# A float32 square in block 0 written for GpSimd instead of ScalarE

## The chip, the cores and the metric

The kernel runs on one core of a Trainium2 chip. Its engines each take their own instructions in order: TensorE (PE in the profile, with its weight loads as PEld), VectorE (DVE), ScalarE (ACT), GpSimd (POOL) and SyncE (SP, which here issues the transfers). [...] The metric is the device time of one execution in microseconds (us), as the median of several.

## The reference

Attention of 8 batches (512 rows of x, 32 of state, 8 heads of 64) gives 4352 + 256 = 4608 rows of 512 numbers; two feed-forward layers follow. The change lies in the first of them:

```
def _moe_ref(x, w_in, w_out):        # x: 4608 x 512, w_in: 512 x 2048, w_out: 2048 x 512
    h = x @ w_in
    r = np.maximum(h, 0.0)
    g = r * r
    return g @ w_out
```

The second layer has an elu in place of the squared relu. The weights come as float64 and everything is computed to float32 accuracy: each product of two float32 matrices is made of three products of parts, a part HI rounded for TensorE and a rest LO = value - HI.

## The kernel before

The first layer runs block by block, one block being one batch (512 columns of x, transposed). Blocks 0 to 3 go through `s1_step` and `out_step`; blocks 4 to 7 and everything later go through other code, with products saved by sums of parts. A block has 16 steps f. In step f, `s1_x` makes h(f) from six matmuls of 128x512 into PSUM, `relu2` turns h(f) into the pair gs (HI and LO), and `out_step` takes the gs of two steps earlier (LAG = 2) as the moving side of twelve matmuls into the four accumulators `acc`. gs has three buffers, r and g have one each.

`relu2` (L583 to L591) has four instructions: L585, ScalarE, r = relu(h) out of PSUM; L587, ScalarE, g = r squared, float32; L589, ScalarE, gs[HI] = r squared, rounded; L590, VectorE, gs[LO] = g - gs[HI].

Block 0 is special, since the weights are turned from float64 to float32 beside it (`convert`, L222 to L241). The 8 pieces of w1 and 8 of v1 each have a tile of 128x1024: ScalarE makes the high part (L232) and the low part (L234) out of the loaded words, a clamp follows (L237: on VectorE for w1, on GpSimd for v1 but its first piece), then VectorE shifts (L238) and adds the low part (L241). Pieces of v1 are then split into HI (L260 on ScalarE or L258 on VectorE) and LO (L262 on VectorE). Three pieces are done before the first step, the other 13 are spread over steps 0 to 14. The converted w1 is wanted by `emit_m` (products with the state into m, split by L177 and L178) and the converted v1 by `out_step`. The attention of batch 1 is worked on beside it too (L392 to L506, L527 to L542).

What one engine does in which order is settled when the program is built: a scheduler orders the instructions by their dependences, with the conversions of a step tied to its relu by `pace`, so that a change of one line can move its neighbours. On the chip each engine then goes through its list in order.

## Time and profile before

| | us |
|---|---|
| median of 3 runs (1308.95 to 1310.94) | 1310.32 |
| the profiled execution, whole | 1313.85 |
| its span from first to last instruction | 1312.1 |
| TensorE busy in the span | 1292.2 |
| VectorE busy | 945.4 |
| ScalarE busy | 835.5 |
| GpSimd busy | 8.8 |

"Busy" is the time in which an engine had at least one instruction in work. TensorE is busy nearly all the time, so what counts is where it isn't. About 25 us of the span go by before the first step; block 0's conversions fill the stretch from 25.7 to 97.2 us. Instruction records on one engine overlap by some 0.08 us, as the next one starts while the last one drains.

### The profile page before, as it was taken

What the parts mean: (1) busy time and instruction counts of PE and PEld (TensorE: products, weight loads), DVE (VectorE), ACT (ScalarE), POOL (GpSimd) and SP (SyncE); (2) the same over time, 40 slices, a digit from 0 to 9 for tenths busy, and PEclk for the clock granted to TensorE, in tenths of its full rate; (3) what the DMA queues carried; (4) which work ended last, traced back from release to release, by engine and by line L of the source; (5) the groups of instructions that cost most, each with busy time, mean ns of one, the idle gap of its engine ahead of it and who ended that gap; (6) DMA issues with size and microseconds to landing.
All of it is one profiled execution on the core that took longest, in us unless ns stands there. A gap on an engine that the chain in (4) does not pass through costs nothing.

```text
span 1312.1 us, 19392 instructions
## 1 busy us (share of the span) xinstructions
PE 1292.2 (98%) x6964; PEld 1036.4 (79%) x6964; DVE 945.4 (72%) x1327; ACT 835.5 (64%) x1347; POOL 8.8 (1%) x13
## 2 busy tenths in 40 slices
PE   7989999999999999999999999999999999999999
PEld 5667777777677777779988888888888888888898
DVE  6996968687769865985767963789546984568644
ACT  6886778677765667665577644685446743666444
POOL 0110000000000000000000000000000000000000
PEclk9999999999999999999999999999999999999999
DMA  9889888786825653589686678767786777678733
GB/s 370 312 301 336 314 288 303 260 302 234 276 96 156 192 186 117 178 281 360 216 261 195 201 209 264 224 191 211 221 276 194 208 210 233 200 211 282 227 103 110
DMA packets 135408, 305.39 MB, mean 233 GB/s; under 512 B 14352, under 2 KB 28688, under 8 KB 132240
## 3 DMA queue, kind: packets, MB, share of 16 engines
q1 hardware_dynamic: 135312, 304.14, 70.9%
q8 instruction: 56, 0.92, 0.3%
q14 instruction: 40, 0.33, 0.1%
HBM read 227.54 MB, written 76.55 MB: 232 GB/s over the span
## 4 chain that ended last, share of the span: by engine, by line
PE 85%; DVE 5%; issue 5%; DMA 2%; ACT 2%; POOL 1%; POOLq 0%; SPq 0%; DVEq 0%; ACTq 0%
PE x L43 19%; PE X L43 13%; PE z L43 10%; PE Z L43 7%; PE y L43 4%; PE h L170 4%; PE h L172 4%; PE h L171 4%; PE acc L170 3%; PE Y L43 3%; PE acc L172 3%; PE acc L171 3%; PE as L43 2%; PE mp L362 2%; PE hs L43 1%
## 5 line engine op out<-in xcount | busy, mean ns | idle before, releaser
L178 DVE TENSOR_TENSOR gp<-g,gp 128x512 fp32r<-128x512 f32 (+1 forms) x224 | 212.4, 955 | 107.1 <-ACT gp L177 106.1
L177 ACT ACTIVATE gp<-g 128x512 fp32r<-128x512 f32 (+1 forms) x224 | 187.7, 843 | 155.6 <-PE x L43 78.2
L43 PE MATMUL x<-gp,wr 128*128 128x512 f32 x1152 | 272.7, 391 | 1.0 <-ACT eu L71 1.0
L43 PEld LDWEIGHTS x<-gp,wr 128*128 128x128 f32 x1152 | 215.1, 188 | 51.6 <-ACT eu L71 2.9
L43 PE MATMUL X<-xf,wr 128*128 128x512 f32 x768 | 186.6, 390 | 0.0
L43 PEld LDWEIGHTS X<-xf,wr 128*128 128x128 f32 x768 | 143.5, 188 | 31.5 <-ACT u L957 1.1
L43 PE MATMUL z<-gp,wr 128*128 128x512 f32 x576 | 133.5, 390 | 0.0
L43 PEld LDWEIGHTS z<-gp,wr 128*128 128x128 f32 x576 | 108.0, 188 | 23.4 <-issue 0.8
L953 DVE SCALAR_TENSOR_TENSOR g<-r,g 128x512 f32<-128x512 f32 x96 | 63.9, 689 | 62.8 <-ACT r L952 62.8
L170 PE MATMUL acc<-gs,v 128*128 128x512 f32 x256 | 103.9, 406 | 4.1 <-DVE gs L590 3.4
L170 PE MATMUL h<-at,m 128*128 128x512 f32 x256 | 101.8, 398 | 0.7 <-ACT m L177 0.7
L172 PE MATMUL h<-at,m 128*128 128x512 f32 x256 | 99.8, 392 | 1.5 <-DVE m L178 1.5
L171 PE MATMUL acc<-gs,v 128*128 128x512 f32 x256 | 100.1, 391 | 0.0
L171 PE MATMUL h<-at,m 128*128 128x512 f32 x256 | 99.9, 390 | 0.0
L172 PE MATMUL acc<-gs,v 128*128 128x512 f32 x256 | 99.4, 392 | 0.4 <-DVE v L262 0.4
L43 PE MATMUL Z<-xf,wr 128*128 128x512 f32 x384 | 97.4, 389 | 0.0
L951 ACT ACTIVATE r<-g 128x512 f32<-128x512 f32 x96 | 57.6, 625 | 58.6 <-DVE g L1001 41.6
L81 DVE TENSOR_TENSOR g<-g,g 128x1024 f32<-128x1024 f32 x72 | 87.5, 1220 | 0.8
L43 PEld LDWEIGHTS Z<-xf,wr 128*128 128x128 f32 x384 | 72.1, 188 | 15.0
L952 ACT ACTIVATE r<-r 128x512 f32<-128x512 f32 x136 | 81.6, 621 | 0.7
L170 PEld LDWEIGHTS acc<-gs,v 128*128 128x128 f32 x256 | 48.0, 188 | 31.4 <-issue 10.1
L43 PE MATMUL y<-gp,wr 128*128 128x512 f32 x288 | 68.6, 389 | 0.0
(166 smaller groups left out, 1994.7 us busy)
## 6 DMA issues: line engine op xcount, KB each, us to landing
wr<-f_v SPq DMA_DIRECT2D x288, 256.0 KB, 3.0
wr<-f_w SPq DMA_DIRECT2D x224, 256.0 KB, 3.0
f_v<-wf SPq DMA_DIRECT2D x40, 512.0 KB, 3.6
raw_w<-in_w_dram SPq DMA_DIRECT2D x32, 512.0 KB, 5.3
raw_v<-in_v_dram SPq DMA_DIRECT2D x32, 512.0 KB, 6.5
f_w<-wf SPq DMA_DIRECT2D x24, 512.0 KB, 3.7
wr<-p_v SPq DMA_DIRECT2D x48, 256.0 KB, 3.5
xt<-in_xt_dram SPq DMA_DIRECT2D x8, 1024.0 KB, 6.0
```

The lines of the kernel that those rows point to most:

```text
L43: nc.tensor.matmul(ps, wk[a], xk[b], start=start and k == 0 and i == 0, stop=last and k == len(w) - 1 and i == 2, skip_group_check=True)
L81: return lambda jj: tt(out=out[jj], in0=a[jj], in1=b[jj], op=ALU.subtract)
L170: mm(ps, w[HI], x[LO], start=first, stop=False)
L171: mm(ps, w[HI], x[HI], start=False, stop=False)
L172: mm(ps, w[LO], x[HI], start=False, stop=last)
L177: copy = nc.scalar.activation(out=hi, in_=src, func=AF.Copy)
L178: lows[:] = [nc.vector.tensor_tensor(out=lo, in0=src, in1=hi.bitcast(F32), op=ALU.subtract)]
L362: mm(ps[e][32 * k:32 * k + 32, :], st_t[b][r, k, :], x(k, r), start=True, stop=True)
L951: act(out=r, in_=h, func=AF.Relu, scale=-1.0)
L952: act(out=r, in_=r, func=AF.Exp, scale=-1.0)
L953: nc.vector.scalar_tensor_tensor(out=out, in0=r, scalar=-1.0, in1=h, op0=ALU.add, op1=ALU.max)
```

## The change

`relu2` is told its block. In block 0 the float32 square g is no longer ScalarE's: GpSimd multiplies r by r. ScalarE keeps the rounded square gs[HI], and VectorE's subtraction takes g from GpSimd. Blocks 1 to 3 are as before. Behind the new lines all line numbers are 3 higher (L589 becomes L592, L590 becomes L593).

```diff
-        def relu2(ps, n):
+        def relu2(ps, n, b):
             r = g_p.tile([P, n], F32, name="r", tag="r")
             pace[:] = [nc.scalar.activation(out=r, in_=ps, func=AF.Relu)]
             g = g_p.tile([P, n], F32, name="g", tag="g")
-            nc.scalar.activation(out=g, in_=r, func=AF.Square)
+            if b:
+                nc.scalar.activation(out=g, in_=r, func=AF.Square)
+            else:
+                nc.gpsimd.tensor_tensor(out=g, in0=r, in1=r, op=ALU.mult)
             gs = gs_p.tile([P, 2, n], F32R, name="gs", tag="gs")
             nc.scalar.activation(out=gs[:, HI], in_=r, func=AF.Square)
             nc.vector.tensor_tensor(out=gs[:, LO], in0=g, in1=gs[:, HI].bitcast(F32), op=ALU.subtract)
...
-            waiting.append((b, f, relu2(ps, S)))
+            waiting.append((b, f, relu2(ps, S, b)))
```

On ScalarE, at step 1 of block 0 (cv and raw_v are a piece of v1; a wait on Pool_49 is one for GpSimd):

```order
-L585 ACTIVATE r<-h 128x512 [waits PE_49,Activation_49]
+L585 ACTIVATE r<-h 128x512 [waits PE_49,Activation_49,Pool_49]
 L232 ACTIVATE cv<-raw_v_154 128x1024 [waits DMAHW2_49,DMAHW0_49]
-L587 ACTIVATE g<-r 128x512 [waits DVE_49,Activation_49]
-L589 ACTIVATE gs<-r 128x512
+L592 ACTIVATE gs<-r 128x512 [waits Activation_49]
 L234 ACTIVATE raw_v_154<-raw_v_154 128x1024
```

The square L587 is gone from the row between L232 and the rounded square, and the next relu now waits for GpSimd to have read r.

On VectorE, at steps 1 and 2 of block 0 (cv is a piece of v1, w_3 one of w1):

```order
+L593 TENSOR_TENSOR gs<-g,gs 128x512 [waits Activation_49,Pool_49]
 L238 TENSOR_SCALAR cv<-cv 128x1024 [waits Pool_49]
-L590 TENSOR_TENSOR gs<-g,gs 128x512 [waits Activation_49]
+L542 COPY stf<-srt_435 64x4x32 [waits PE_49]
 L241 ISA cv<-raw_v_154,cv 128x2048 [waits DMAHW0_49,DMAHW2_49,DVE_49,Activation_49]
-L542 COPY stf<-srt_435 64x4x32 [waits PE_49]
-L237 TENSOR_SCALAR w_3_429<-w_3_429 128x1024 [waits Activation_49]
+L593 TENSOR_TENSOR gs<-g,gs 128x512 [waits Activation_49,Pool_49]
+L237 TENSOR_SCALAR w_3_429<-w_3_429 128x1024
```

The subtraction waits for GpSimd as well as for ScalarE, and it stands ahead of the shift L238, which waits for GpSimd's clamp, and not behind it.

On GpSimd, the start of its list in the changed kernel (before, the clamps L237 stand there alone, seven in a row):

```order
+L590 TENSOR_TENSOR g<-r 128x512 [waits Activation_49]
+L590 TENSOR_TENSOR g<-r 128x512 [waits DVE_49,Activation_49]
+L237 TENSOR_SCALAR cv<-cv 128x1024 [waits Activation_49]
+L590 TENSOR_TENSOR g<-r 128x512 [waits DVE_49,Activation_49] x2
+L237 TENSOR_SCALAR cv<-cv 128x1024 [waits Activation_49]
```

Sixteen squares now stand among the seven clamps, most often two squares and then a clamp; each square waits for r from ScalarE and for VectorE to have read the last g.

## Rows read from the trace of the kernel before

**Rows 1.** The page: busy time, share of the span and instructions of each engine.

```profile
PE 1292.2 (98%) x6964; PEld 1036.4 (79%) x6964; DVE 945.4 (72%) x1327; ACT 835.5 (64%) x1347; POOL 8.8 (1%) x13
```

**Rows 2.** Busy time by stretch: stretch, length, engines, granted clock, DMA share, GB/s.

```profile
core 0: us, PE busy (x) PEld busy (x) DVE busy (x) ACT busy (x) POOL busy (x), PEclk, DMA share, GB/s
25.70:97.20 71.50, 66.10 (x452) 45.76 (x451) 64.65 (x87) 65.11 (x94) 8.13 (x7) 1.00 0.87 315
97.20:1312.10 1214.90, 1207.34 (x6402) 977.02 (x6400) 865.72 (x1218) 756.39 (x1234) 0.00 (x0) 1.00 0.70 225
```

**Rows 3.** Waits from 25.7 to 97.2 us: who for whom, total, times, longest.

```profile
PE acc L170 <- DVE gs L590: 3.4, 6, 1.2
PE srt L540 <- DVE m L178: 0.9, 1, 0.9
PE acc L172 <- DVE v L262: 0.4, 1, 0.4
PE h L172 <- DVE m L178: 0.4, 1, 0.4
PE acc L170 <- ACT v L260: 0.3, 1, 0.3
...
DVE cv L238 <- POOL cv L237: 4.6, 5, 1.3
DVE w L237 <- ACT w L232: 1.4, 1, 1.4
DVE gs L590 <- ACT gs L589: 0.3, 1, 0.3
```

**Rows 4.** ScalarE's groups, same stretch: count, busy us, mean ns, idle before.

```profile
L587 ACT ACTIVATE g<-r 128x512 f32<-128x512 f32 x15 | 9.7, 644 | 0.1
```

**Rows 5.** GpSimd in order of time: start, us, instruction, idle before it.

```profile
32.19 1.04 POOL L237 TENSOR_SCALAR cv<-cv 128x1024 f32<-128x1024 f32 x1 [30.89 <-ACT cv L232]
...
59.73 1.04 POOL L237 TENSOR_SCALAR cv<-cv 128x1024 f32<-128x1024 f32 x1 [7.48 <-ACT cv L232]
73.77 1.88 POOL L237 TENSOR_SCALAR cv<-cv 128x1024 f32<-128x1024 f32 x1 [12.99 <-ACT cv L232]
82.86 1.04 POOL L237 TENSOR_SCALAR cv<-cv 128x1024 f32<-128x1024 f32 x1 [7.22 <-ACT cv L232]
```

**Rows 6.** VectorE in order of time, around 59.7 and 73.8 us.

```profile
59.50 1.21 DVE L490 TENSOR_REDUCE m<-t 128x32 f32<-128x1024 f32 x1
...
73.55 1.18 DVE L241 CUSTOM_DVE_ANT_0 w<-raw_w,w 128x2048 uint16<-128x2048 uint16 x1
74.76 1.42 DVE L590 TENSOR_TENSOR gs<-g,gs 128x512 fp32r<-128x512 f32 x1
```

**Rows 7.** VectorE's groups by form from 25.7 to 97.2 us.

```profile
L590 DVE TENSOR_TENSOR gs<-g,gs 128x512 fp32r<-128x512 f32 x14 | 10.3, 739 | 0.5 <-ACT gs L589 0.3
L262 DVE TENSOR_TENSOR v<-cv,v 128x1024 fp32r<-128x1024 f32 x8 | 9.8, 1220 | 0.0
L241 DVE CUSTOM_DVE_ANT_0 cv<-raw_v,cv 128x2048 uint16<-128x2048 uint16 x8 | 9.8, 1219 | 0.1
L241 DVE CUSTOM_DVE_ANT_0 w<-raw_w,w 128x2048 uint16<-128x2048 uint16 x6 | 7.3, 1212 | 0.0
L238 DVE TENSOR_SCALAR cv<-cv 128x1024 int32<-128x1024 int32 x8 | 5.5, 692 | 4.6 <-POOL cv L237 4.6
...
L238 DVE TENSOR_SCALAR w<-w 128x1024 int32<-128x1024 int32 x6 | 4.1, 690 | 0.1
L237 DVE TENSOR_SCALAR w<-w 128x1024 f32<-128x1024 f32 x6 | 4.1, 686 | 1.5 <-ACT w L232 1.4
...
L258 DVE CAST v<-cv 128x1024 fp32r<-128x1024 f32 x2 | 1.3, 672 | 0.0
...
L501 DVE TENSOR_TENSOR t<-t,z 128x1024 f32<-128x1024 f32 x1 | 1.2, 1225 | 0.0
L491 DVE TENSOR_TENSOR t<-t,m 128x1024 f32<-128x1024 f32 x1 | 1.2, 1218 | 0.0
```

**Rows 8.** ScalarE in order of time, step 1 of block 0.

```profile
30.45 0.61 ACT L585 ACTIVATE r<-h 128x512 f32<-128x512 f32 x1
30.92 1.18 ACT L232 ACTIVATE cv<-raw_v 128x1024 f32<-128x1024 f32 x1
31.97 0.66 ACT L587 ACTIVATE g<-r 128x512 f32<-128x512 f32 x1
32.49 0.65 ACT L589 ACTIVATE gs<-r 128x512 fp32r<-128x512 f32 x1
```

**Rows 9.** VectorE in order of time, the last subtractions of block 0.

```profile
102.26 0.69 DVE L590 TENSOR_TENSOR gs<-g,gs 128x512 fp32r<-128x512 f32 x1 [1.55 <-ACT gs L589]
106.34 0.69 DVE L590 TENSOR_TENSOR gs<-g,gs 128x512 fp32r<-128x512 f32 x1 [3.39 <-ACT gs L589]
```

## The prediction

> **What bounds the kernel now.** I read the page first: TensorE is busy 98% of the span, every other engine far less [rows 1], so a change away from TensorE can only matter where TensorE stands still. The busy time by stretch shows where that is [rows 2]. From 97.2 us to the end TensorE is idle 1214.9 - 1207.34 = 7.6 us in 1215; from 25.7 to 97.2 us, which is block 0 with the conversion of the weights, it is idle 71.5 - 66.1 = 5.4 us, at full clock (1.00). The squares that the change moves all lie in block 0. In that stretch three engines are nearly equally full: TensorE 66.1, ScalarE 65.1, VectorE 64.65 of 71.5 us. GpSimd has 8.1 us of work. Whichever of the three is made slower by a few us sets the stretch, and what is lost there is not won back, because TensorE has no slack behind it.

> Next the waits of the same stretch [rows 3]. TensorE waits for VectorE: 3.4 us for the subtraction L590, 0.9 and 0.4 for m, 0.4 for v; for ScalarE only 0.3. VectorE in its turn is idle 71.5 - 64.65 = 6.85 us, and the large waits behind that are 4.6 us for GpSimd's clamp, 1.4 for ScalarE's L232 and 0.3 for ScalarE's rounded square. So the last link before TensorE is VectorE, and ScalarE's lateness reaches TensorE only through VectorE's 6.3 us of waits.

> **What is removed.** ScalarE loses L587 in each of the 16 steps; 15 of them lie in the stretch with 9.7 us of records [rows 4], and a square moves its successor by 0.52 us (L589 starts 0.52 after L587 [rows 8]), so in 14 steps some 14 x 0.52 = 7.3 us of ScalarE's time. That cannot shorten the stretch by 7.3: TensorE has only 5.4 us to give, and VectorE, the last link, gains at most its 6.3 us of waits.

> **What is added, alone.** GpSimd gets 16 products of 128x512. None is in the trace. The nearest row is its clamp of 128x1024, 1.04 us when undisturbed [rows 5]: that reads 1024 numbers per partition, and a product of two 512-long inputs reads as many. Below, half of it (0.52) if r counted once; above, two passes like the clamp's (2.08). I take 1.04, the row with the same number of reads. [...] GpSimd then has 8.1 + 14 x 1.04 = 22.7 us in 71.5: it is not itself full.

> **What is added, beside VectorE.** One clash in the trace shows that the two engines don't run freely beside each other. At 73.77 the clamp starts while VectorE is in L241 (73.55, 1.18); the clamp takes 1.88 instead of 1.04, and the L590 that comes at 74.76 takes 1.42 [rows 5, 6] where 0.69 is usual [rows 9]. So the clamp stood until L241 was through and L590 stood until the clamp was through: 0.84 lost on one side, 0.73 on the other. At 59.73 a clamp runs beside L490, a reduction with one input, and both keep their time (1.04, 1.21) [rows 5, 6]. So GpSimd shuts out VectorE's operations with two inputs in SBUF and is shut out by them; one-input ones at the slow rate are free.

> How much of VectorE's time is of the excluding kind [rows 7]? The groups of the stretch add up to 69.7 us of records for 64.65 of busy time, a factor 0.93. With two SBUF inputs: L590 10.3, L262 9.8, L241 9.8 and 7.3, L491 and L501 1.2 each, 39.6 in all, so 36.7 us. The quick one-input operations L238 (5.5, 4.1), L237 (4.1) and L258 (1.3) are 15.0, so 13.9 us. No clamp meets one of these in the rows. They pass 1024 numbers in 0.69 us, where the reduction L490 needs 1.21, so they read at the rate of a two-input operation, and I count them as excluding. The rest is 15 us of records: reductions, transposes and L178, which has one input in PSUM. [...]

> So GpSimd finds VectorE in an excluding operation for (36.7 + 13.9) / 71.5 = 0.71 of the time, or 36.7 / 71.5 = 0.51 if the quick ones don't count. Each square that lands there costs VectorE about its own length. Of 16 squares 14 lie in the stretch; the last two fall where VectorE waits 1.55 and 3.39 us for its input [rows 9], and cost nothing. The term: 14 x 1.04 x 0.71 = **10.3 us** of VectorE (7.5 with the smaller share).

> **What moves.** VectorE's list has the subtraction ahead of the shift L238, no longer behind it. That uses part of the 4.6 us in which VectorE stood waiting for a clamp [rows 3]. Against it, a clamp now queues behind a square on GpSimd: in step 1, r is ready at 31.06 and L232, which releases the clamp, at 32.10 [rows 8], 1.04 later, exactly a square that starts at once; whatever a square is held up, the clamp behind it is late by, and with it L238 and L241. Also the square waits for VectorE to have read the last g (one buffer), and the relu for GpSimd to have read r; I take both as free, since each of the two is done within the step. Of VectorE's 6.3 us of waits I let half go, **3.2 us**: all of it is the bound if ScalarE's lead reaches every clamp, none if the squares eat the lead. No transfer is removed or added; those that wait for converted tiles come earlier or later with them.

> **Sum.** 10.3 - 3.2 = +7.1 us of VectorE. Before, VectorE's 64.65 us of work and 6.85 of idle made 71.5; now about 75 of work and blocked time and 3.7 idle make 78.6, while TensorE still wants 66.1 and ScalarE falls to some 58. VectorE becomes the bound of block 0, and the 7.1 pass on to the end. The profiled execution of 1313.85 would become 1320.9. It lay 3.5 above the median of the runs, 1310.32; on the median the forecast is 1317.4. The term's ends: with the smaller share and all waits recovered 7.5 - 6.3 = +1.2; with two-pass squares 20.7 - 3.2 = +17.5.

> **Rivals.**
> 1. ScalarE was the true bound, and GpSimd fits in between. For it: ScalarE is as full as VectorE (65.1), it feeds the clamps for which VectorE waits 4.6 us, and VectorE's new order puts gs earlier, which is what TensorE waits for (3.4 us). It needs squares that mostly hit VectorE's idle and free time. Against it: the clash. Its price is a gain of most of TensorE's 5.4 us idle, about 4: 1306.3. It decides if VectorE's blocked time stays below what its waits shrink by.
> 2. Both cancel: the smaller share (7.5) against all of the waits (6.3), or squares that fall into time in which VectorE waits for g anyway. Within 2.6 us of 1310.3.
> 3. Slower still: GpSimd gets no turn between back-to-back VectorE operations. In the clash L241 was followed by a VectorE pause for its input, so the rows don't show who wins when the next operation is ready. If VectorE always does, a square starts only when VectorE stands at the subtraction that wants it, and each costs its whole 1.04 and a start of some 0.09 (from the end of L232 at 32.10 to its clamp at 32.19 [rows 5, 8]): 14 x 1.13 = 15.8, less 3.2: +12.6, 1322.9. It decides if squares show as 2 us and more, with VectorE idle before L593.

> **How the numbers follow.** The forecast, slower by some 7 us, has 0.48, its own range is 1311.5 to 1322; rival 1 has 0.20, rival 2 0.18, rival 3 0.14. What a measurement can tell from no change here is about 0.2%, 2.6 us. Slower by more: 0.45 of the forecast's 0.48 (its lower end lies within the 0.2%) and all of rival 3, 0.59. Within: 0.18 + 0.03 = 0.21. Faster: 0.20. The range from 1306 to 1325 leaves out half of rival 1 and a part of rival 3.

> **What would show it.** In the profile after: GpSimd's squares with a median well over 1.04 us; L593, L241, L262 and L238 with longest records over 1.2 to 2 us and a larger mean; VectorE's busy time in block 0 near 75 us and its waits for GpSimd larger, now before L593; ScalarE at about 58; TensorE's idle time in block 0 near 12 us, and the time from block 1 on unchanged. I am wrong if squares and VectorE keep their undisturbed lengths, or if TensorE's idle time there falls below 5.4.

## The result: slower by 0.9%, as forecast in kind

The changed kernel takes 1321.76 us (median of four runs, 1319.86 to 1325.09), the kernel before 1309.88 us in the same comparison (1308.95 to 1310.94). The ratio is 1.0093 with a 95% interval of 1.0074 to 1.0111: 11.9 us slower, where 7.1 us were forecast and 1306 to 1325 us was the range. A second set of runs of the same kernel, below, gave 1319.35 us and 9.5 us. So the sign and the stretch were right, and the size was too small by 2.4 to 4.8 us.

The profiled execution took 1319.86 us with a span of 1317.9 us; that of before had 1313.85 and 1312.1. By the page, TensorE is still the engine that is always busy, GpSimd has 25 us more of records, and ScalarE has 7.8 us less, against [rows 1]:

```profile
PE 1294.6 (98%) x6964; PEld 1037.3 (79%) x6964; DVE 957.0 (73%) x1327; ACT 827.7 (63%) x1331; POOL 33.8 (3%) x29
```

The next rows are the busy times of stretches of the changed kernel: start and end, length, then each engine with its instructions, the granted clock, the DMA share. The first is the stretch of [rows 2]. Since the work of block 0 now takes longer, the same clock time holds less of it (TensorE 60.74 us for 66.10), so the stretch to compare ends at the first copy of block 0's accumulator: 121.59 us here, 111.62 before. The third row is what follows it.

```profile
25.70:97.20 71.50, 60.74 (x343) 42.02 (x341) 66.08 (x76) 51.13 (x69) 26.79 (x18) 0.93 0.75 272
...
25.70:121.59 95.89, 84.93 (x526) 59.42 (x525) 81.83 (x99) 63.66 (x90) 33.12 (x23) 0.95 0.79 285
...
121.59:1317.90 1196.31, 1191.21 (x6328) 964.50 (x6326) 860.05 (x1206) 749.96 (x1223) 0.00 (x0) 1.00 0.69 225
```

The same stretches of the kernel before:

```profile
25.70:111.62 85.92, 80.52 (x526) 56.75 (x525) 70.33 (x99) 71.63 (x107) 8.13 (x7) 1.00 0.88 319
...
111.62:1312.10 1200.48, 1192.91 (x6328) 966.03 (x6326) 860.05 (x1206) 749.88 (x1223) 0.00 (x0) 1.00 0.70 224
```

Block 0 ends 10.0 us later. VectorE has the same 99 instructions and needs 81.83 us for them instead of 70.33: 11.5 us more, all of it time in which an instruction stood. Its idle time shrank from 15.6 to 14.1 us. ScalarE fell by 8.0 us. TensorE's idle time rose from 5.4 to 11.0 us, and its busy time by 4.4 us, of which some 3.2 go with the granted clock (0.95 for 1.00): the same kernel at full clock, further below, has 81.75 us for 84.93. Behind block 0 nothing changed that can be told from the spread of single executions: 1196.3 us here, 1200.5 in the profiled execution of before, which was a long one (1313.85 against a median of 1309.88), and 1195.5 to 1200.4 in the ten other profiles of this document in which blocks 1 to 3 are as before.

Waits of the changed kernel from 25.7 to 97.2 us, answering [rows 3]: who for whom, us in total, times, longest.

```profile
PE acc L170 <- DVE gs L593: 2.8, 3, 1.8
...
PE acc L172 <- DVE v L262: 2.6, 2, 1.4
...
DVE v L262 <- ACT v L260: 2.3, 1, 2.3
...
PE mp L362 <- DVE w L241: 1.8, 2, 1.2
PE acc L170 <- DVE v L258: 1.7, 1, 1.7
...
POOL g L590 <- DVE gs L593: 1.4, 2, 0.7
...
DVE gs L593 <- POOL g L590: 0.9, 1, 0.9
```

VectorE no longer waits for clamps (4.6 us before), and it waits for squares only 0.9 us here (2.0 to the end of block 0). It waits less than before and works more slowly; and TensorE now waits for everything that VectorE makes, the converted tiles v and w (L262, L258, L241) as much as the subtraction.

How it becomes slow is seen in GpSimd's groups (count, busy us, mean ns), against clamps of 1.04 us undisturbed [rows 5]:

```profile
L590 POOL TENSOR_TENSOR g<-r 128x512 f32<-128x512 f32 x16 | 21.3, 1329 | 77.7 <-ACT r L585 72.3 <-DVE tf L276 3.3 <-DVE gs L593 2.1
L237 POOL TENSOR_SCALAR cv<-cv 128x1024 f32<-128x1024 f32 x7 | 12.0, 1719 | 0.0
```

and in GpSimd and VectorE in order of time (start, us, instruction). GpSimd:

```profile
30.53 2.13 POOL L590 TENSOR_TENSOR g<-r 128x512 f32<-128x512 f32 x1 [2.03 <-ACT r L585]
32.64 2.01 POOL L237 TENSOR_SCALAR cv<-cv 128x1024 f32<-128x1024 f32 x1
...
60.81 1.04 POOL L590 TENSOR_TENSOR g<-r 128x512 f32<-128x512 f32 x1 [2.18 <-ACT r L585]
...
76.90 1.04 POOL L590 TENSOR_TENSOR g<-r 128x512 f32<-128x512 f32 x1 [13.60 <-ACT r L585]
```

VectorE at the same moments:

```profile
30.55 1.22 DVE L262 TENSOR_TENSOR v<-cv,v 128x1024 fp32r<-128x1024 f32 x1
31.68 2.06 DVE L241 CUSTOM_DVE_ANT_0 w<-raw_w,w 128x2048 uint16<-128x2048 uint16 x1
33.67 1.52 DVE L593 TENSOR_TENSOR gs<-g,gs 128x512 fp32r<-128x512 f32 x1
...
60.86 1.53 DVE L258 CAST v<-cv 128x1024 fp32r<-128x1024 f32 x1
...
76.94 2.08 DVE L501 TENSOR_TENSOR t<-t,z 128x1024 f32<-128x1024 f32 x1
```

### The profile page after: what moved, and what is told of

Read it like the earlier page. It is cut to its first block, busy times and chain, and to the rows that moved or that the text cites. A ratio compares the mean times of both kernels' runs of the same rounds, so it can differ in the third digit from the quotient of the medians.

```text
span 1317.9 us, 19404 instructions
## 1 busy us (share of the span) xinstructions
PE 1294.6 (98%) x6964; PEld 1037.3 (79%) x6964; DVE 957.0 (73%) x1327; ACT 827.7 (63%) x1331; POOL 33.8 (3%) x29
## 4 chain that ended last, share of the span: by engine, by line
PE 83%; DVE 4%; DMA 2%; ACT 2%; issue 1%; SPq 0%; ACTq 0%; DVEq 0%
PE x L43 19%; PE X L43 13%; PE z L43 10%; PE Z L43 7%; PE y L43 4%; PE h L170 4%; PE h L172 4%; PE h L171 4%; PE Y L43 3%; PE acc L170 3%; PE acc L172 3%; PE acc L171 3%; PE as L43 2%; PE mp L362 2%; PE hs L43 1%; DMA f_v<-wf 1%
## 5 line engine op out<-in xcount | busy, mean ns | idle before, releaser
L178 DVE TENSOR_TENSOR gp<-g,gp 128x512 fp32r<-128x512 f32 (+1 forms) x224 | 212.4, 955 | 106.3 <-ACT gp L177 105.4
L170 PE MATMUL acc<-gs,v 128*128 128x512 f32 x256 | 104.8, 409 | 5.3 <-DVE gs L593 2.8
L172 PE MATMUL acc<-gs,v 128*128 128x512 f32 x256 | 101.3, 400 | 2.6 <-DVE v L262 2.6
L171 PE MATMUL acc<-gs,v 128*128 128x512 f32 x256 | 100.9, 394 | 0.0
L170 PEld LDWEIGHTS acc<-gs,v 128*128 128x128 f32 x256 | 48.6, 190 | 33.1 <-issue 11.7
L585 ACT ACTIVATE r<-h 128x512 f32<-128x512 f32 x64 | 38.0, 594 | 51.6 <-PE h L172 51.6
```

Source lines behind the costliest of these rows:

```text
L170: mm(ps, w[HI], x[LO], start=first, stop=False)
L171: mm(ps, w[HI], x[HI], start=False, stop=False)
L172: mm(ps, w[LO], x[HI], start=False, stop=last)
L178: lows[:] = [nc.vector.tensor_tensor(out=lo, in0=src, in1=hi.bitcast(F32), op=ALU.subtract)]
L585: pace[:] = [nc.scalar.activation(out=r, in_=ps, func=AF.Relu)]
```

## Experiments: does what GpSimd reads set the price?

My theory was that the time lost is VectorE's time shut out by GpSimd's reads of SBUF, the on-chip memory (the expectations call it a shared port, a name for the theory: the runs show lengths of instructions, not a port); the rival was that the new order and the new dependency (the subtraction waits for GpSimd) cost it, whatever the instruction does. The first two kernels have VectorE's, ScalarE's, TensorE's and SyncE's instructions in the order of the changed kernel; only GpSimd's instruction differs. The first keeps the dependencies, too; in the second GpSimd no longer waits for r, nor ScalarE's relu for GpSimd. The rows quoted below are always the stretch from 25.7 us to the first copy of block 0's accumulator.

**One read instead of two.**

```diff
-                nc.gpsimd.tensor_tensor(out=g, in0=r, in1=r, op=ALU.mult)
+                nc.gpsimd.tensor_scalar(out=g, in0=r, scalar1=CLAMP, scalar2=-CLAMP, op0=ALU.min, op1=ALU.max)
```

> GpSimd's instruction in block 0 clamps r into g (a one-input operation of the same kind as its clamp of the weights) where the changed kernel multiplies r by r; it leaves out the float32 square, and the lists of the four other engines stay word for word those of the changed kernel. Theory (the read port that GpSimd and VectorE share): what costs is the time in which GpSimd reads, so an instruction of 512 reads, about 0.52 us undisturbed, blocks VectorE half as long; 14 x 0.52 x 0.71 = 5.2 us less 3.2 of waits: 1 to 6 us above the kernel before, against 11.9 for the changed kernel. Rival (the new order of VectorE's list and the hand-over between three engines cost the time): nothing of that changes, so about 12 us stay.

1316.15 against 1310.21 us, ratio 1.0049 [1.0034, 1.0064]: 5.9 us slower, half of the change's 11.9.

```profile
25.70:118.33 92.63, 84.05 (x528) 59.30 (x527) 77.47 (x100) 63.77 (x90) 25.90 (x23) 0.96 0.81 295
```

**No read at all.**

```diff
-                nc.gpsimd.tensor_tensor(out=g, in0=r, in1=r, op=ALU.mult)
+                nc.gpsimd.memset(g, 0.0)
```

> GpSimd's instruction in block 0 fills g with zeros, without reading r; it leaves out the float32 square, and the lists of the four other engines stay word for word those of the changed kernel. Theory (shared read port): an instruction that reads nothing doesn't hold VectorE's two-input operations, so VectorE keeps its lengths (means near 0.69 and 1.22 us), and what is left is the relief of ScalarE: from 4 us faster than the kernel before to 2 slower. Rival (order and hand-over): about 12 us slower, as the changed kernel.

1313.16 against 1310.21 us, ratio 1.0023 [1.0013, 1.0032]: 2.95 us slower, a little above my range, far from the rival's 12.

```profile
25.70:113.52 87.82, 81.50 (x528) 57.00 (x527) 74.93 (x100) 63.63 (x91) 25.51 (x22) 1.00 0.86 312
```

**The product twice.**

```diff
                 nc.gpsimd.tensor_tensor(out=g, in0=r, in1=r, op=ALU.mult)
+                nc.gpsimd.tensor_tensor(out=g, in0=r, in1=r, op=ALU.mult)
```

> The changed kernel with GpSimd's product made twice into the same g. Theory (shared port): another 14 x 1.04 x 0.7 = 10 us of blocked VectorE, so 20 to 26 us above the kernel before, with more time at the lower granted clock. Rival (order and hand-over): the second product only lengthens the way to g, for which two steps of lag have room: 12 to 15 us.

1333.47 against 1310.21 us, ratio 1.0183 [1.0167, 1.0200]: 23.3 us slower.

```profile
25.70:134.51 108.81, 87.89 (x526) 60.19 (x525) 86.97 (x99) 64.02 (x90) 57.50 (x39) 0.92 0.70 254
```

The kernels together: with 0, 512, 1024 and 2048 numbers read per partition and step, the kernel is 2.95, 5.9, 9.5 to 11.9 and 23.3 us slower than before, and VectorE's busy time in block 0 is 74.93, 77.47, 81.4 to 81.8 and 86.97 us. Undisturbed, the memset and the clamp of r are of nearly one length (0.53 and 0.61 us), and the one that reads costs twice as much. The rival wanted 12 us from both; it falls with the clamp of r, whose order and dependencies are those of the change.

Only up to 1024 does the price follow the reads, though. Against the two profiles of the change the second product adds 5.1 to 5.5 us to VectorE's busy time, but 7.8 to 9.2 us to its idle time (108.81 - 86.97 = 21.8 us, after 14.1 and 12.6): the subtraction now waits for the second product, 10.3 us in block 0 after 2.0 and 2.3. So more than half of what the second product costs is the hand-over that the rival named.

## Experiments: what the relief and the order are worth

**No square at all.** The subtraction reads r, and neither engine makes g.

```diff
-                nc.gpsimd.tensor_tensor(out=g, in0=r, in1=r, op=ALU.mult)
+                g = r
```

> Block 0 has no float32 square at all: VectorE subtracts the rounded square from r. This leaves out g, and so is the relief of ScalarE alone, without a burden on GpSimd. Theory (VectorE is the last link before TensorE): VectorE loses only part of its 6.3 us of waits, so 1 to 4 us faster than the kernel before. Rival 1 of the prediction (ScalarE is the bound of block 0): 4 to 5.4 us faster, TensorE's idle time there near nothing.

1311.81 against 1310.21 us, ratio 1.0012 [1.0003, 1.0022]: 1.6 us slower. Both expectations missed; each had a gain.

```profile
25.70:112.25 86.55, 80.41 (x526) 56.64 (x525) 73.58 (x99) 63.94 (x90) 10.14 (x7) 1.00 0.85 314
```

and the groups of that subtraction and of the clamp (count, busy us, mean ns):

```profile
L593 DVE TENSOR_TENSOR gs<-r,gs 128x512 fp32r<-128x512 f32 x16 | 14.9, 933 | 3.0 <-ACT gs L592 3.0
...
L237 POOL TENSOR_SCALAR cv<-cv 128x1024 f32<-128x1024 f32 x7 | 10.1, 1449 | 80.5 <-ACT cv L232 80.5
```

ScalarE has 7.7 us less to do, and block 0 ends 0.6 us later. VectorE's idle time fell from 15.6 to 13.0 us, so 2.6 us of its waits were indeed won back; but its busy time rose by 3.25 us with no square anywhere. The two group rows show why. VectorE's list is close to that of the changed kernel, though not the same: the subtraction stands ahead of the shift, that is, just where a clamp runs on GpSimd: the clamps take 1449 ns on the average instead of 1161 (8.13 / 7), the subtraction 933 instead of 730. The shift used to wait for the clamp in idle time; the subtraction fills this time and is shut out by the clamp. Six of the 16 subtractions start while a clamp runs, and these six take 0.98 to 1.53 us. What the order gives, the clash takes.

**The reverse: squares without relief.** The kernel before, with one product more on GpSimd that nobody reads. VectorE's list in block 0 is that of before.

```diff
             nc.scalar.activation(out=g, in_=r, func=AF.Square)
+            if b == 0:
+                x = g_p.tile([P, n], F32, name="x", tag="x")
+                nc.gpsimd.tensor_tensor(out=x, in0=r, in1=r, op=ALU.mult)
```

> The kernel before, with ScalarE's square kept, and GpSimd making a second one of r in block 0 that nobody reads. Theory (shared port): VectorE is blocked as in the changed kernel, and ScalarE isn't relieved: 8 to 16 us above the kernel before. Rival (what costs is that VectorE has to wait for GpSimd's g): VectorE waits for nothing new, so 0 to 2 us.

1317.10 against 1310.03 us, ratio 1.0056 [1.0041, 1.0071]: 7.1 us slower, 0.9 below the lower end of my expectation, far above the rival's.

```profile
25.70:119.50 93.80, 82.04 (x528) 57.21 (x528) 78.75 (x100) 72.25 (x106) 32.42 (x23) 1.00 0.82 291
```

Products that feed nothing cost VectorE 78.75 - 70.33 = 8.4 us, and block 0 ends 7.9 us later. This is the disputed cost by itself. It can be counted in the trace: of the first 14 products 10 hold up an instruction of VectorE, eight with two inputs in SBUF, one L237 and one L238, and each of these ten takes 0.82 to 0.86 us longer than usual. One of them, GpSimd's line first (L241 usually takes 1.22):

```profile
99.32 1.10 POOL L590 TENSOR_TENSOR x<-r 128x512 f32<-128x512 f32 x1 [1.13 <-ACT r L585]
99.44 2.06 DVE L241 CUSTOM_DVE_ANT_0 cv<-raw_v,cv 128x2048 uint16<-128x2048 uint16 x1
```

With the 3.25 us of the kernel without squares it makes 11.7 us, against 11.5 and 11.1 us measured in the two profiles of the change. That the two costs simply add is not shown, since the lists of the two kernels differ from that of the change; in the trace of the change three subtractions stand behind a clamp (1.52, 1.52 and 1.32 us), some 2.3 us.

**The same square on VectorE.**

```diff
-                nc.gpsimd.tensor_tensor(out=g, in0=r, in1=r, op=ALU.mult)
+                nc.vector.tensor_tensor(out=g, in0=r, in1=r, op=ALU.mult)
```

> In block 0 VectorE itself makes the float32 square, 0.61 us each, GpSimd none. Theory (shared port): 14 x 0.61 = 8.5 us of VectorE less about 3 of waits: 4 to 8 us above the kernel before, so less than the 11.9 that the product costs on GpSimd. Rival (VectorE has room, GpSimd was merely late): no more than 2 us above.

1319.33 against 1310.03 us, ratio 1.0071 [1.0056, 1.0086]: 9.3 us slower, a little over the expected 4 to 8.

```profile
25.70:119.46 93.76, 83.36 (x525) 58.48 (x524) 83.34 (x115) 63.96 (x91) 9.13 (x7) 0.96 0.85 306
```

with the squares as a group of VectorE:

```profile
L590 DVE TENSOR_TENSOR g<-r 128x512 f32<-128x512 f32 x16 | 11.7, 734 | 1.6 <-ACT r L585 1.5
```

The squares are 11.7 us of records; VectorE's busy time rises by 13.0 us, and the kernel loses 9.3. With GpSimd making them VectorE's busy time rises by 11.1 to 11.5 us and the kernel loses 9.5 to 11.9. Here the idle engine relieved nobody: VectorE paid nearly as much for GpSimd's squares as for its own, and the kernel no less.

**Half of the squares.**

```diff
-            if b:
+            if b or f % 2:
                 nc.scalar.activation(out=g, in_=r, func=AF.Square)
```

> Only the even steps of block 0 have their square on GpSimd, the odd ones on ScalarE. Theory (shared port): half of the blocked time, 5 us, and half of the relief: 2 to 5 us above the kernel before; if TensorE's pauses stay short enough for the clock to hold, less than half of the 11.9. Rival (one hand-over too many in the chain, whatever its number): 8 us and more.

1314.75 against 1310.03 us, ratio 1.0033 [1.0021, 1.0045]: 4.7 us slower, as the theory had it. VectorE's busy time up to the first copy of the accumulator rises by 5.8 us, half of the 11.1 to 11.5 of all squares. The loss goes with the number of squares here; other numbers were not tried.

**The clamps on VectorE.** If GpSimd's reads cost VectorE as much as its own work, the clamps that the kernel before has there should be worth nothing either.

```diff
-            clamp = nc.gpsimd if name == "v1" and i else nc.vector
+            clamp = nc.vector
```

> The kernel before with its seven clamps of v1 on VectorE, too, so that GpSimd does nothing in block 0. VectorE gets 7 x 0.61 = 4.3 us of work and loses 4.6 us of waits for a clamp and the 0.73 of the one clash. Theory (a one-input operation on GpSimd that VectorE waits for is worth about what it costs): within 3 us of the kernel before. Rival (VectorE's work alone counts, waits are free): 4 us slower or more.

1311.99 against 1309.83 us, ratio 1.0021 [1.0011, 1.0031]: 2.2 us slower.

```profile
25.70:112.31 86.61, 80.91 (x526) 56.98 (x526) 74.19 (x107) 71.61 (x107) 0.00 (x0) 1.00 0.90 322
```

VectorE's busy time rises by 3.9 us and block 0 ends 0.7 us later, in an execution that was among the shorter ones (1310.98): taken back, the seven clamps move the time by 0.2%, as I expected (within 3 us). That they are worth a little on GpSimd agrees with where they lie: before, VectorE stood waiting for most of them (4.6 us [rows 3]).

## Experiments: other blocks

**Blocks 1 to 3 instead of block 0.** There VectorE is busy only 178.19 of 220.49 us before the change, so I expected the squares to find room.

```diff
-            if b:
+            if b == 0:
                 nc.scalar.activation(out=g, in_=r, func=AF.Square)
```

> The edit turned round: block 0 as before, GpSimd makes the 48 float32 squares of blocks 1 to 3. Theory (GpSimd's reading costs only where VectorE is the last link): TensorE is never idle there and VectorE has a fifth of its time free, so within 3 us of the kernel before, though VectorE's records lengthen as in block 0. Rival (each product on GpSimd costs the same wherever it is): 3 x 11.9 = 36 us slower.

1326.38 against 1310.03 us, ratio 1.0121 [1.0104, 1.0138]: 16.3 us slower. Both missed. Blocks 1 to 3, and 12 us inside them:

```profile
111.32:349.14 237.82, 226.42 (x1319) 170.68 (x1319) 200.96 (x326) 141.01 (x245) 56.74 (x46) 0.97 0.76 267
...
190.00:202.00 12.00, 5.70 (x16) 3.79 (x15) 12.00 (x17) 6.96 (x12) 3.81 (x3) 0.69 0.69 220
```

and the three blocks of the kernel before:

```profile
111.62:332.11 220.49, 219.79 (x1315) 166.69 (x1313) 178.19 (x325) 164.13 (x290) 0.00 (x0) 1.00 0.80 287
```

The mean share of 81% hid stretches in which VectorE has no room: from 190 to 202 us it is busy 12.00 of 12.00, and TensorE 5.70. Before the change VectorE is as full there: in the 8 us up to the copies of block 1's accumulator (180 to 188 us) it is busy 7.97 of 8.00, while TensorE still gets 7.83. Over the three blocks VectorE's busy time grows by 22.8 us. The blocks take 17.3 us longer: TensorE's idle time grows from 0.7 to 11.4, and its busy time by 6.6 at a mean granted clock of 0.97 for 1.00 (0.69 in the 12 us shown, with TensorE idle for more than half of them).

**Was it the one buffer of r?** ScalarE's relu waits there for GpSimd to have read r (total, times, longest):

```profile
ACT r L585 <- POOL g L590: 8.5, 7, 3.0
```

So the same kernel with r in a pool of its own of two buffers:

```diff
+    r_p = pool("r", 2)
...
-            r = g_p.tile([P, n], F32, name="r", tag="r")
+            r = r_p.tile([P, n], F32, name="r", tag="r")
```

> The squares of blocks 1 to 3 on GpSimd, as in the run that took 16 us more than the kernel before, with two buffers for r instead of one. There ScalarE's relu waited 8.5 us for GpSimd to have read the last r, with all that is queued behind it on ScalarE. Theory (the single r ties ScalarE to a GpSimd that is held up by VectorE): half of the 16 us or more goes, 2 to 8 above the kernel before. Rival (VectorE's blocked time counts there, too): 13 us or more stay.

1327.24 against 1309.83 us, ratio 1.0135 [1.0120, 1.0151]: 17.4 us slower, no better, although the relu now waits only 1.6 us for GpSimd. The one buffer of r is not the reason; the rival, VectorE's blocked time, stands. The one buffer of g, for which GpSimd waits 26.9 us in these blocks, was not tried, and how the 16 us are shared out among VectorE's stretches stays open.

## Experiments: the clock, and how steady the size is

**The changed kernel once more,** nothing edited.

> The changed kernel once more, beside the next one on the same chip. Between its first four executions the span went with the mean granted clock: 1317.9 us at 0.995, 1317.5 at 0.994, 1321.3 at 0.992, 1323.1 at 0.991. Theory (part of the loss is TensorE at half clock after it stood still in block 0): 9 to 14 us above the kernel before, and the spans again fall as the clock rises, some 1.3 us for each 0.001. Rival (VectorE's blocked time is all, the clock is a sign of it): spans that don't follow the clock.

1319.35 against 1309.83 us, ratio 1.0075 [1.0060, 1.0090]: 9.5 us slower, at the lower end of what was expected. The spans follow the clock, but less than expected: 1316.3 to 1318.7 us at 0.997 to 0.993, some 0.6 us for each 0.001, and the two at 0.998 are longer than the one at 0.997. Its profiled execution:

```profile
25.70:119.78 94.08, 81.75 (x526) 56.73 (x525) 81.44 (x99) 63.81 (x90) 33.76 (x23) 1.00 0.81 290
```

This one ran block 0 at the full granted clock, and block 0 ended 8.2 us later than before instead of 10.0: VectorE's busy time +11.1, its idle time -3.0. In the first profile TensorE fell to half clock there. Busy times of the changed kernel, first profile, in steps of 2 us (the last three columns are granted clock, DMA share and GB/s), and TensorE in order of time:

```profile
64.00:66.00 2.00, 0.97 (x2) 0.84 (x3) 2.00 (x3) 0.00 (x0) 0.00 (x0) 0.50 0.95 375
66.00:68.00 2.00, 2.00 (x6) 1.58 (x5) 2.00 (x3) 0.00 (x0) 0.00 (x0) 0.50 0.81 330
```

```profile
62.45 0.50 PE L170 MATMUL acc<-gs,v 128*128 128x512 f32 x1 [1.72 <-DVE v L258]
...
65.03 1.22 PE L172 MATMUL acc<-gs,v 128*128 128x512 f32 x2 [1.38 <-DVE v L262]
66.05 0.63 PE L170 MATMUL acc<-gs,v 128*128 128x512 f32 x1
66.48 0.63 PE L171 MATMUL acc<-gs,v 128*128 128x512 f32 x1
...
70.72 0.39 PE L172 MATMUL acc<-gs,v 128*128 128x512 f32 x1
70.95 0.39 PE L170 MATMUL acc<-gs,v 128*128 128x512 f32 x1
```

TensorE had waited 1.72 us for L258 and then stood 1.38 us for L262; during this second wait the granted clock fell, from 1.00 (63.5 to 63.8 us) to 0.50 (64 to 70 us), and from then on matmuls follow each other every 0.43 us instead of 0.23, until 70.7; from 71 us on the clock is 1.00 again. There is a second such piece from about 91 to 94.5 us (0.50 from 92 to 94 us). TensorE's busy time is 84.93 - 81.75 = 3.2 us longer than in the second profile, and the end of block 0 is 1.8 us later. All of that comes from the first piece: the matmul after the wait for L262 starts at 65.03 in the first profile and at 65.02 in the second, the next square at 76.90 and 75.06, the last one at 111.12 and 109.31. What made the clock fall is not shown: in the second profile TensorE waited at the same two places 0.82 and 2.22 us, as long in sum, and stayed at 1.00.

**TensorE kept from standing still.** In the steps 1 to 15 of block 0, four matmuls of zeros onto the accumulator.

```diff
+            for i in range(4 if b == 0 and f else 0):
+                mm(acc[i][:, :P], zeros, ident, start=False, stop=False, skip_group_check=True)
```

> The changed kernel with four small products of a zero matrix (128x128) added to the accumulators ahead of out_step's matmuls in steps 1 to 15 of block 0, so that TensorE does something in the time in which it waits for VectorE; the sums don't change. Theory (half clock has a price of its own): the granted clock of the executions rises to 0.997 to 0.999, the stretches at half clock in block 0 get fewer, and although TensorE has 60 more matmuls it takes 1 to 5 us less than the changed kernel. Rival (clock without a price): as the changed kernel or up to 7 us slower.

1330.97 against 1309.83 us, ratio 1.0161 [1.0146, 1.0176]: 21.1 us slower.

```profile
25.70:131.10 105.40, 96.21 (x643) 74.35 (x642) 78.93 (x99) 64.03 (x91) 33.59 (x23) 0.94 0.78 283
```

Both expectations missed. The fill made TensorE 96.21 - 81.75 = 14.5 us busier in block 0, more than the 12.3 us in which it stood idle, so it took the place of work; and the granted clock still fell (0.94). So this doesn't tell what the clock alone costs; that rests on the comparison of the two profiles of the same kernel.

## Why the prediction held, point by point

- **The bound.** The page and the busy times by stretch put the risk into block 0 and onto VectorE, with nothing won back later. So it was: 8.2 and 10.0 us of the loss stand at the end of block 0, and the rest of the span is 1196.3 and 1197.3 us, beside 1196.4 for a run of before with the median time, if its block 0 ends alike (span 1308.0 less 111.62). The two profiles are of executions of 1319.9 us; those of 1323.4 and 1325.1 us, which raise the median to 11.9 us above before, have no profile.
- **What ScalarE is relieved of.** 7.3 us expected, 7.7 to 8.0 measured (71.63 to 63.94, 63.81 and 63.66). That it can't shorten the stretch by as much was right, but I still let 3.2 us of it reach VectorE: with the squares left out altogether block 0 ended 0.6 us later.
- **The product alone.** 1.04 us, taken from the clamp with the same number of reads: the least disturbed squares take 1.04. Right.
- **The exclusion, 10.3 us.** For the squares alone this was too much: products added to the old order cost VectorE 8.4 us. The share was right, the price of a meeting was not. 10 of 14 products, 0.71, met VectorE in an excluding operation; each cost it 0.82 to 0.86 us and not the 1.04 that the product lasts, and the clash that I had read showed 0.73. That the quick one-input operations belong on the list was my estimate from their rate (1024 numbers in 0.69 us), shown by no row of before; the trace of after shows it: L258 (1.53), L237 (1.53) and L238 (1.37 and 1.53) all stand beside a square or clamp there, where 0.65 to 0.70 us is usual. One reading of the rows was wrong: of L178 only the products m have an input in PSUM, the two records of at (1.4 us) have both in SBUF and belonged there, too.
- **What moves, -3.2 us.** The half of VectorE's waits that I let go was nearly right (3.0 us in the second profile, 1.5 in the first, 2.6 without squares). **The step that failed** is that this was taken as free: the subtraction in the clamp's place is itself shut out by the clamp. That is 3.25 us of VectorE, seen without any square, and some 2.3 us in the trace of the change (one subtraction, 0.73, before); it has no term in my sum. It was luck that this and the dear exclusion nearly cancel: 8.4 + 3.25 - 2.6 = 9.1, where 10.3 - 3.2 = 7.1 stood; 8.2 was measured at full clock.
- **The clock.** Not in the sum, and it should have been: I let TensorE's idle time grow from 5.4 to 12 us (12.3 and 11.0 measured) without asking what the granted clock does in a stretch with such gaps. It is the difference between the two profiles, 1.8 us. The runs of the first comparison have mean clocks of 0.995 to 0.991 and spans of 1317.5 to 1323.1 us, those of the second 0.998 to 0.993 and 1316.3 to 1318.7. That the clock also makes the rest of the way from 9.5 to 11.9 us is likely by these numbers and not shown.
- **The single buffers,** called free: nearly. Three squares that come right after a clamp wait 0.69 us each for the subtraction to have read g; two buffers of r changed nothing in the other blocks. Two buffers of g were not tried.
- **The signs.** Longer squares (median 1.32 us), longer records of VectorE, ScalarE relieved and TensorE's idle time all came as written. One did not: VectorE's waits for GpSimd were to grow and to stand before L593, and they shrank, from 4.6 us to 2.0 and 2.3.
- **Rival 1** (ScalarE the true bound) falls with the kernel without squares. **Rival 2** (both cancel) wanted 7.5 us of blocked time and all 6.3 us of waits back; 8.4 and at most 3.0 came. **Rival 3** (GpSimd gets no turn) gave 12.6 us, and 11.9 is nearer to that than to my 7.1, but by another mechanism: squares of 2 us and more with VectorE idle before L593 were its mark, and only two of the 16 are so long (median 1.32 us), while VectorE waits 2.0 us for them. The rows at 30.5 us show the engines taking turns, and the pause after L241 that I read into the clash is 0.03 us in the rows (73.55 + 1.18 to 74.76).

## What to carry to other kernels

Before work is moved to an idle GpSimd, ask what VectorE does at that moment: here each product that met two-input work in SBUF or a quick one-input operation (L237, L238) cost VectorE 0.82 to 0.86 us, most of the product's own 1.04, and the whole move cost as much as giving VectorE the work (9.5 to 11.9 us and 9.3). Price the reordering, too: an instruction that moves into a wait moves next to what was being waited for. A mean busy share of 81% says nothing of room; look for the stretches that are full.

## What the runs showed of the hardware that I had not expected

**GpSimd and VectorE take turns in some places and not in others.** From 30.5 to 34.6 us of the changed kernel, where neither engine pauses, each instruction after L262 waits for one of the other engine (2.13, 2.06, 2.01, 1.52 us in a row). Elsewhere they didn't take turns: in the kernel with one read a clamp let two of VectorE's instructions pass, both of which kept their lengths. GpSimd and VectorE:

```profile
52.97 2.76 POOL L237 TENSOR_SCALAR cv<-cv 128x1024 f32<-128x1024 f32 x1
```

```profile
53.01 1.22 DVE L241 CUSTOM_DVE_ANT_0 w<-raw_w,w 128x2048 uint16<-128x2048 uint16 x1
54.14 0.69 DVE L593 TENSOR_TENSOR gs<-g,gs 128x512 fp32r<-128x512 f32 x1
```

The clamp took 2.76 us for 1.04; the longest GpSimd instruction of block 0 took 1.88 us before, 2.13 in the first profile of the change, 2.07 without squares and 2.15 with the memset. What decides who goes next is not shown.

**Writing alone is not free either, but meets other instructions.** In the kernel with the memset, GpSimd and VectorE in order of time:

```profile
37.27 1.01 POOL L590 MEMSET g<- 128x512 f32 x1 [1.55 <-DVE gs L593]
...
57.98 0.53 POOL L590 MEMSET g<- 128x512 f32 x1 [1.99 <-DVE gs L593]
...
77.85 0.53 POOL L590 MEMSET g<- 128x512 f32 x1 [0.60 <-DVE gs L593]
```

```profile
37.13 0.69 DVE L237 TENSOR_SCALAR w<-w 128x1024 f32<-128x1024 f32 x1
...
57.84 0.70 DVE L396 STREAM_TRANSPOSE t<-sc 128x512 f32<-128x512 f32 x1
...
77.72 1.21 DVE L241 CUSTOM_DVE_ANT_0 w<-raw_w,w 128x2048 uint16<-128x2048 uint16 x1
```

A memset takes 0.53 us beside a transpose, and beside the two-input L241, which keeps its 1.21; it takes 1.01 us where a quick one-input operation (L237, L238 or L258) is running, until that one is through. Of the 15 memsets from 25.7 us on the 11 with 1.01 or 1.02 us all start 0.13 to 0.15 us after the start of such an operation, the four with 0.52 or 0.53 do not.

**One operation, two places.** In the trace of the change L178 kept 0.68 us at 106.81, beside the square of 106.41, where one input is in PSUM (m), and took 1.53 us at 98.40, beside the square of 98.26, where both inputs are in SBUF (at).
